# Sliding-window attention followed by a two-layer MLP: a planner that counts engine occupancy and latency apart, no latency between matmuls of one chain, k's copy after q's transposes, identity from the iota

## The chip, the cores and the metric

The kernel runs on one core of one Trainium2 chip. The metric is device microseconds of one execution, as the median over several runs. One execution of each kernel was also profiled. The engines are called PE (TensorE), DVE (VectorE), ACT (ScalarE), POOL (GpSimd) and SP (SyncE).

## The reference, cut to what matters

Eight batches of 576 positions, 8 heads of 64; causal attention in a window of 128 with a linear bias per head, then `relu(x @ w_in)**2 @ w_out` with 512, 2048 and 512 features.

```python
scores = np.matmul(q, k.transpose(0, 1, 3, 2)) / np.sqrt(D)
rel = pos[:, None] - pos[None, :]
mask = (rel >= 0) & (rel < 128)
scores = np.where(mask, scores - slopes[:, None, None] * np.abs(rel), -1e9)   # [B, H, S, S]
attn = softmax(scores)                                                        # cut
x = np.matmul(attn, v).transpose(0, 2, 1, 3).reshape(B * S, H * D)            # 4608 x 512
out = np.square(np.maximum(x @ w_in, 0)) @ w_out                              # 4608 x 512
```

## The kernel before

A block is 128 query positions of one batch (the fifth of each batch has 64), so there are 40 blocks. For each block PE transposes k and q (`tp`), forms scores (`ps_s`), multiplies the probabilities by v (`pv`) and transposes the result (`xp`). For each 512 tokens the MLP makes 16 `h` chains of 4 matmuls and 4 `o` chains of 16. A *chain* here is a row of matmuls that together fill one tile of PSUM, the memory that matmuls write into.

Every instruction group is a `Task`. A list scheduler written in the kernel, `Plan.order`, gives each task a modelled start, and the instructions are recorded in that order. Each engine then works through its instructions in the recorded order on the chip (in the trace of before the 2496 matmuls, 393 instructions of ACT and 579 of DVE stand in the order of the built program); the modelled times themselves do nothing there. The parts that matter:

```python
class Plan:
    LAT = {"PE": 220.0, "ACT": 120.0, "DVE": 120.0, "POOL": 150.0, "SP": 2200.0}
    # ... order(): take the candidate with the earliest start, then the lowest key
                t.end = st + dur + (self.LAT[e] if t.lat is None else t.lat)
            free[e] = st + dur
            # ...
            for u in t.users:
                left[u] -= 1
                u.ready = max(u.ready, t.end)       # also from one matmul of a chain to the next
# ...
    def act(n): return n * 0.833 + 175.0            # ns that ACT is taken
    def dve(n, rate=1): return n / rate / 0.96 + 150.0
    def mm(n): return max(n, 64) / 2.4 + 1.5
# ... attention(m): eight transposes into ONE PSUM tile, k's in its first half, q's in its second
        for i in range(2 * C):
            def emit(i=i):
                # ...
                    slot.tile = psum.tile([128, 1024], BF16, tag=slot.tag, name="tp")
                nc.tensor.transpose(slot.tile[:, i * 128:(i + 1) * 128], ..., ident)
            last = plan.add({"PE": mm(128)}, due - 56, emit, [last, ...], ...)
            if i == C - 1:
                last_k = last
        # ... k's copy, then q's in two halves
        t_k = plan.add(both if first else {"DVE": both["DVE"]}, due - 56, evac_k, [last_k], [], [slot])
        for c2 in range(2):
            t_q.append(plan.add(both if first else {"ACT": both["ACT"]} if c2 else {"DVE": both["DVE"]},
                                due - 56, evac_q, [last, t_zero], [], [slot]))
```

Masks and identity were built on POOL, which also issues all the loads.

The softmax here doesn't subtract the row's maximum and nothing guards it: scores larger than these inputs give would overflow.

## Time and profile before

The time was 366.05 us (median of 3 runs, 364.43 to 366.13). The page's first lines for the kernel before, then its row of PE activity and granted clock in 40 slices of the span (a digit is tenths):

```profile
span 364.2 us, 6535 instructions
...
PE 338.9 (93%) x2496; PEld 187.5 (51%) x2496; DVE 193.8 (53%) x593; ACT 205.1 (56%) x394; POOL 108.4 (30%) x137
...
PE   2677899999999999999999999999999999999995
...
PEclk9996999999999999999999999999999999999999
```

PE is the busy engine, but 93% does not say how much is to be had. The Trainium skill ("Perfetto Trace Analysis", Identifying the Most-Contended Engine) warns that matmul busy time is a poor measure of this, because matmuls are pipelined. So I use another account throughout. At full clock, matmuls of 512, 256, 128 and 65 columns start 216, 110, 56 and 29 ns apart in this trace. At about these pitches (213 for 512) the 2496 matmuls need 317.2 us. **Excess** is what the starts take beyond that:

| stretch, us | excess before, us | named waits of PE in it |
|---|---|---|
| 0 to 60 | 23.3 | loads, copies, exponentials; a clock drop |
| 60 to 300 | 13.6 | 9.7 of it: 29 times a transpose of q waits over 0.1 us for the copy of k |
| after 300 | 1.3 | |

(The prediction counts these waits from 0.2 us on: 27 times and 9.4 us.) With 4.7 us before the first matmul and 4.3 us after the last start, this makes up the span: 4.7 + 317.2 + 38.2 + 4.3 = 364.4 (the last matmul's 0.2 us stand in both 317.2 and 4.3).

The wait of q's transposes is easy to miss. The timeline of PE and DVE at 95 us shows one of them; the columns are start, duration, engine and line, operation, tiles, and shapes:

```profile
95.36 0.22 PE L301 MATMUL tp<-ident,kn_73 128*128 128x128 bf16 x1
95.42 0.38 PE L479 MATMUL o<-w_out_sb,g 128*128 128x512 bf16 x1
...
95.62 0.42 DVE L280 COPY kT_87<-tp 128x512 bf16<-128x512 bf16 x1 [0.23 <-PE tp L301]
95.64 0.38 PE L450 MATMUL h<-xT,w_in_sb 128*128 128x512 bf16 x1
...
96.10 0.22 PE L301 MATMUL tp<-ident,qn_77 128*128 128x128 bf16 x1
```

The `h` matmul that starts at 95.64 is through after 216 ns, at 95.86; the next matmul starts at 96.10, just after the copy of k ends at 96.04. PE lost 0.25 us, and yet no idle time is printed for it, since the modelled duration of the `h` (0.38 us) hides it. Where idle time does show, line 301's view (idle time of its engine, then how often) has it as:

```profile
  DVE kT_86 L280: 1.6, 6
  DVE kT_84 L280: 1.5, 5
  DVE kT_85 L280: 1.0, 4
  DVE kT_87 L280: 0.7, 3
```

That is 4.8 us, where starts show 9.7 in 60 to 300 us alone. The Trainium skill ("PSUM — Partial Sum Buffer", PSUM bank collisions raise a hardware error) says why such a wait is there: engines have to be kept apart by PSUM bank and quarter of the partitions, not by address. k's and q's transposes share one 2 KB tile, and k's copy reads all 128 partitions of it.

### The profile page before, as it was taken

Reading aid. Unit: us, or ns where it says so; the run is one execution under the profiler, and the core shown is the slowest. Engines: PE = TensorE matmul, PEld = TensorE weight load, DVE = VectorE, ACT = ScalarE, POOL = GpSimd, SP = SyncE. Lnnn points to the kernel's source line nnn. Section 1 sums busy time; section 2 is a strip of 40 time slices with the busy share of each in tenths; the row PEclk is TensorE's granted clock in tenths of the full one; section 3 lists DMA queues with packets and bytes.
Section 4 is the critical chain, followed back from the end, with each engine's and each line's share of the span. In section 5 each row is a group of like instructions: output and inputs, shape, how many; then the busy total and the mean of one; then the engine's idle time right before and its main releaser. Section 6 shows DMA issues by size and latency. Waiting matters only on the chain.

```text
span 364.2 us, 6535 instructions
## 1 busy us (share of the span) xinstructions
PE 338.9 (93%) x2496; PEld 187.5 (51%) x2496; DVE 193.8 (53%) x593; ACT 205.1 (56%) x394; POOL 108.4 (30%) x137
## 2 busy tenths in 40 slices
PE   2677899999999999999999999999999999999995
PEld 1454555555555555555555555564555555444442
DVE  4583776476656744566466745664656554322200
ACT  4582775476656754576557645675656643343411
POOL 8967552352444322233243213240100000000000
PEclk9996999999999999999999999999999999999999
DMA  8999999695997967986497777791432000001012
GB/s 56 144 203 160 195 172 86 88 79 60 86 102 51 82 65 76 113 81 40 51 98 70 73 72 75 71 88 36 57 47 38 29 31 31 29 29 58 31 58 87
DMA packets 121951, 28.21 MB, mean 77 GB/s; under 512 B 113216, under 2 KB 117312, under 8 KB 121920
## 3 DMA queue, kind: packets, MB, share of 16 engines
q0 software_dynamic: 116736, 18.36, 68.3%
q1 hardware_dynamic: 5184, 9.44, 7.1%
q8 instruction: 19, 0.31, 0.3%
q14 instruction: 12, 0.10, 0.1%
HBM read 36.70 MB, written 9.44 MB: 127 GB/s over the span
## 4 chain that ended last, share of the span: by engine, by line
PE 76%; issue 7%; POOL 5%; DMA 4%; DVE 4%; ACT 2%; POOLq 0%; ACTq 0%
PE h L450 30%; PE o L479 30%; PE ps_s L337 6%; PE tp L301 5%; PE pv L378 4%; DMA kn_71<-in_k_dram 3%; PE xp L417 2%; DMA qn_74<-in_q_dram 1%; DVE kT_86 L280 1%; DVE kT_87 L280 1%; DVE kT_84 L280 1%; DVE kT_85 L280 1%; POOL w_in_sb L238 1%; POOL kn_70 L262 1%; POOL vt_79 L262 0%
## 5 line engine op out<-in xcount | busy, mean ns | idle before, releaser
L450 PE MATMUL h<-xT,w_in_sb 128*128 128x512 bf16 x576 | 199.4, 382 | 0.7 <-ACT xT L282 0.5
L479 PE MATMUL o<-w_out_sb,g 128*128 128x512 bf16 x576 | 190.8, 379 | 0.2
L458 ACT ACTIVATE rt<-h 128x512 bf16<-128x512 f32 x144 | 85.4, 597 | 84.9 <-PE h L450 69.4
L464 DVE TENSOR_TENSOR g<-rt 128x512 bf16<-128x512 bf16 x144 | 59.8, 419 | 51.3 <-ACT rt L458 49.9
L479 PEld LDWEIGHTS <-g 128*128 128x128 bf16 x576 | 55.2, 98 | 36.0 <-issue 4.7
L450 PEld LDWEIGHTS <-w_in_sb 128*128 128x128 bf16 x576 | 54.8, 98 | 34.8 <-issue 7.0
L399 DVE RECIPROCAL rec<-pv 128x4 f32<-128x4 f32 (+1 forms) x80 | 14.4, 179 | 35.7 <-PE pv L378 34.1
L490 ACT ACTIVATE osb<-o 128x512 f32<-128x512 f32 x36 | 21.5, 596 | 20.7 <-PE o L479 19.9
L355 ACT ACTIVATE P_91<-ps_s 128x512 bf16<-128x512 f32 (+1 forms) x56 | 27.1, 505 | 8.8 <-PE ps_s L337 8.5
L355 ACT ACTIVATE P_92<-ps_s 128x512 bf16<-128x512 f32 (+1 forms) x52 | 26.3, 518 | 8.2 <-PE ps_s L337 7.4
L355 ACT ACTIVATE P_93<-ps_s 128x512 bf16<-128x512 f32 (+1 forms) x52 | 25.9, 515 | 7.2 <-PE ps_s L337 6.5
L378 PEld LDWEIGHTS <-P_91 128*128 128x128 bf16 x200 | 19.1, 98 | 14.4 <-DVE x_94 L404 0.7
L378 PEld LDWEIGHTS <-P_92 128*128 128x128 bf16 x192 | 18.8, 101 | 12.4 <-issue 2.2
L378 PEld LDWEIGHTS <-P_93 128*128 128x128 bf16 x184 | 17.7, 97 | 12.4 <-issue 1.7
L363 DVE TENSOR_TENSOR P_91<-P_91,masks 128x512 bf16<-128x512 bf16 (+1 forms) x56 | 19.7, 361 | 6.5 <-ACT P_91 L355 6.2
L363 DVE TENSOR_TENSOR P_93<-P_93,masks 128x512 bf16<-128x512 bf16 (+1 forms) x52 | 18.7, 365 | 4.8 <-ACT P_93 L355 4.4
L363 DVE TENSOR_TENSOR P_92<-P_92,masks 128x512 bf16<-128x512 bf16 (+1 forms) x52 | 18.4, 365 | 4.9 <-ACT P_92 L355 4.4
L280 DVE COPY xT<-xp 128x512 bf16<-128x512 bf16 (+1 forms) x37 | 14.6, 395 | 8.2 <-PE xp L417 5.8
L417 PE MATMUL xp<-ident,x_94 128*128 128x128 bf16 x80 | 17.5, 224 | 0.0
L417 PE MATMUL xp<-ident,x_95 128*128 128x128 bf16 x80 | 17.1, 223 | 0.0
L404 DVE TENSOR_TENSOR x_94<-pv,rec 128x256 bf16<-128x256 f32 (+1 forms) x40 | 16.7, 416 | 0.5
L262 POOL DMA_DIRECT2D kn_73<-in_k_dram x10 | 8.4, 844 | 28.3 <-PE tp L301 20.9
(99 smaller groups left out, 514.3 us busy)
## 6 DMA issues: line engine op xcount, KB each, us to landing
out_dram<-osb SPq DMA_DIRECT2D x36, 256.0 KB, 2.0
w_in_sb<-in_moe_w_in_dram POOLq DMA_DIRECT2D x4, 512.0 KB, 8.7
w_out_sb<-in_moe_w_out_dram POOLq DMA_DIRECT2D x4, 512.0 KB, 10.8
kn_70<-in_k_dram POOLq DMA_DIRECT2D x8, 128.0 KB, 3.8
qn_74<-in_q_dram POOLq DMA_DIRECT2D x8, 128.0 KB, 4.0
kn_71<-in_k_dram POOLq DMA_DIRECT2D x8, 128.0 KB, 3.6
qn_75<-in_q_dram POOLq DMA_DIRECT2D x8, 128.0 KB, 3.8
kn_72<-in_k_dram POOLq DMA_DIRECT2D x8, 128.0 KB, 3.5
```

What stands on the lines that cost most here:

```text
L280: nc.vector.tensor_copy(o, i)
L301: nc.tensor.transpose(slot.tile[:, i * 128:(i + 1) * 128], src[:, (i % C) * 128:(i % C + 1) * 128], ident)
L337: nc.tensor.matmul(slot_s.tile.rearrange("p (c t q) -> p c t q", c=2, t=2)[:, :, part, 0:n], kT[sk_of[mk].idx][:, c, :], qp[sq.idx][:, c, ...
L355: nc.scalar.activation(view(Pt[sP.idx][:, 2 * c:2 * c + 2]), view(slot_s.tile.rearrange("p (c t q) -> p c t q", c=2, t=2)), AF.Exp, bias=0 ...
L363: nc.vector.tensor_tensor(pt, pt, view(masks[:, 2 * c:2 * c + 2]), op=ALU.mult)
L378: nc.tensor.matmul(slot_v.tile[:, hi * (D + 1):(hi + 1) * (D + 1)], Pt[sP.idx][:, h, part, :], vt[s_in[mk, "v"].idx][:, h, :], start=part ...
L417: nc.tensor.transpose(slot_x.tile[:, c * 128:(c + 1) * 128], xt[sx.idx][:, c * 128:(c + 1) * 128], ident)
L450: nc.tensor.matmul(slot.tile, w_in_sb[:, cc, fc * 128:(fc + 1) * 128], xT[:, cc, g * 512:(g + 1) * 512], start=cc == 0, stop=cc == C - 1)
L458: nc.scalar.activation(srt.tile, slot.tile, AF.Relu, bias=0.0, scale=1.0)
L464: nc.vector.tensor_tensor(sg.tile[:, fc, :], srt.tile, srt.tile, op=ALU.mult)
L479: nc.tensor.matmul(slot.tile, sg.tile[:, fc, t * 128:(t + 1) * 128], w_out_sb[:, fc, :], start=fc == 0, stop=fc == FCB - 1)
L490: nc.scalar.activation(so.tile, slot.tile, AF.Copy)
```

## The change

The intent: let the planner's numbers say what the trace says (how long an engine is *taken*, and how long until a result can be *used*, apart), stop counting latency between matmuls of one chain, start q's transposes without waiting for k's copy, and relieve POOL at the start. In what follows I call the parts A (copy of k), B (planner numbers), C (chain rule) and D (masks and identity).

```diff
-    LAT = {"PE": 220.0, "ACT": 120.0, "DVE": 120.0, "POOL": 150.0, "SP": 2200.0}
+    LAT = {"PE": 260.0, "ACT": 220.0, "DVE": 220.0, "POOL": 200.0, "SP": 2200.0}     # B
+    BEGIN = {"POOL": 1250.0}                                                          # B
-                free.setdefault(e, 0.0)
+                free.setdefault(e, self.BEGIN.get(e, 800.0))                          # B
-                u.ready = max(u.ready, t.end)
+                u.ready = max(u.ready, st + dur if e == "PE" and "PE" in u.engs else t.end)  # C
-        return n * 0.833 + 175.0
+        return n * 0.84 + 55.0                                                        # B
-        return n / rate / 0.96 + 150.0
+        return n / rate / 0.96 + 72.0                                                 # B
-        make_identity(nc, ident)                       # on POOL
-        ... iota and two affine_select on POOL
+        nc.gpsimd.iota(dist, ...)                                                     # D
+        nc.vector.tensor_single_scalar(ident, dist[:, 1], 0.0, op=ALU.is_equal)
+        ... four DVE operations on dist
-            if i == C - 1:
-                last_k = last
-        t_k = plan.add(..., due - 56, evac_k, [last_k], [], [slot])
+        t_k = plan.add(..., due - 56, evac_k, [last], [], [slot])                     # A
-            t1 = plan.add({"DVE": 180.0}, ...
+            t1 = plan.add({"DVE": 97.0}, ...                                          # B
```

More of the change, by code (lines that the diff above doesn't have):

```diff
@@ L6 @@
 import concourse.tile as tile
-from concourse.masks import make_identity
 from concourse._compat import with_exitstack
@@ L160 @@
     dist = const.tile([128, 2, 128], FP32)
+    far = const.tile([128, 2, 128], FP32)
     w_in_sb = const.tile([128, C, d_ff], BF16)
@@ L181, in act, with build_iota, build_ident @@
     def act(n):
-        return n * 0.833 + 175.0
+        return n * 0.84 + 55.0
     def dve(n, rate=1):
-        return n / rate / 0.96 + 150.0
+        return n / rate / 0.96 + 72.0
     def mm(n):
         return max(n, 64) / 2.4 + 1.5
-    def build_consts():
-        make_identity(nc, ident)
-    t_ident = plan.add({"POOL": 800.0}, -9e5 + 0.015, build_consts)
-    def build_dist():
-        pat = [[-128, 2], [1, 128]]
-        nc.gpsimd.iota(dist, pattern=pat, base=128, channel_multiplier=-1,
-                       allow_small_or_imprecise_dtypes=True)
-        nc.gpsimd.affine_select(dist, dist, pattern=pat, channel_multiplier=-1, base=128,
-                                compare_op=ALU.is_ge, fill=1.0e6)
-        nc.gpsimd.affine_select(dist, dist, pattern=[[128, 2], [-1, 128]], channel_multiplier=1,
-                                base=window - 1 - 128, compare_op=ALU.is_ge, fill=1.0e6)
-    t_dist = plan.add({"POOL": 1300.0}, -9e5 + 0.5, build_dist)
+    def build_iota():
+        nc.gpsimd.iota(dist, pattern=[[-128, 2], [1, 128]], base=128, channel_multiplier=-1,
+                       allow_small_or_imprecise_dtypes=True)
+    t_iota = plan.add({"POOL": 360.0}, -9e5 + 0.012, build_iota)
+    def build_ident():
+        nc.vector.tensor_single_scalar(ident, dist[:, 1], 0.0, op=ALU.is_equal)
+    t_ident = plan.add({"DVE": 230.0}, -9e5 - 1, build_ident, [t_iota])
+    def build_dist():
+        mid = (window - 1) / 2.0
+        nc.vector.tensor_single_scalar(far, dist, -mid, op=ALU.add)
+        nc.vector.tensor_tensor(far, far, far, op=ALU.mult)
+        nc.vector.tensor_scalar(far, far, (mid + 0.5) ** 2, 1.0e6, op0=ALU.is_gt, op1=ALU.mult)
+        nc.vector.tensor_tensor(dist, dist, far, op=ALU.add)
+    t_dist = plan.add({"DVE": 1300.0}, -9e5 + 0.5, build_dist, [t_ident])
     t_mask = []
@@ L312, in attention @@
         both = {"ACT": act(C * n), "DVE": dve(C * n, 2)}
-        t_k = plan.add(both if first else {"DVE": both["DVE"]}, due - 56, evac_k, [last_k], [], [slot])
+        t_k = plan.add(both if first else {"DVE": both["DVE"]}, due - 56, evac_k, [last], [], [slot])
         t_q = []
@@ L399, in rec @@
                 nc.vector.reciprocal(srec.tile[0:n, :], pv[0:n, :, D])
-            t1 = plan.add({"DVE": 180.0}, due - 12 + 4 * hf, rec, [last], [srec])
+            t1 = plan.add({"DVE": 97.0}, due - 12 + 4 * hf, rec, [last], [srec])
             def norm(slot_v=slot_v, srec=srec, hf=hf):
```

## The prediction

> **What bounds the kernel.** TensorE. The busy table gives PE 93% of the 364.2 us span, DVE 53%, ACT 56%. In the timeline warm matmuls start 216 ns (512 columns), 110 (256), 56 (128) and 29 ns (65) apart; the Trainium skill ("TensorE: Matmul & The Clock Gate", Back-to-back issue gap) gives N/2.4 + 2.5 ns, which agrees. The 2496 matmuls at about these pitches sum to 317.2 us. The rest of the span: 4.7 us before the first, 4.3 us after the last, 38.3 us of excess between starts. By stretch: 11.1 us before 20 us, 5.1 in 20-30, 4.6 in 30-40, 2.4 in 40-60, 13.6 in 60-300, 1.4 after.
>
> **What the change does.**
> 1. Copy of k after q's transposes. k and q transposes share one 2 KB PSUM tile; before, the copy was recorded between them, so q's transposes wait for it. The Trainium skill ("PSUM — Partial Sum Buffer", PSUM bank collisions) says why such a wait exists. The trace shows PE idle "tp <- DVE kT" 27 times in 60-300 us, 9.4 us together and about 3 us more before. In the built program after no q transpose waits for DVE or ACT. k's copy now starts later, but the first score matmul stands at least 1.28 us of matmul work behind the last transpose from the sixth block on (median over 5 us), so this is mostly hidden. Gain about 10 us, critical.
> 2. Planner durations. Trace: ACT 128x512 starts every 493 ns (model 601 before, 485 after), DVE 128x512 every 334 (417 before, 339 after), last h matmul's start to relu's start 476 ns (213+260 after). The new model fits. Chains run unbroken: the 8 transposes span 0.44 us of PE work instead of 2.1; the first o stands after all 64 first-group h (30 before). This helps the first stage, bounded by latency.
> 3. Identity from the iota, mask distances on DVE. POOL loses a memset and three selects: between q's and the next load it goes from 1.8 us to about 0.5, so all later loads are issued about 1.3 us earlier. DVE gains five small operations (an estimated 1.3 us) while it would wait for data. First transpose near 4.7 us as before (then limited by k's landing, 4.64).
>
> First-stage effect of 2 and 3: first h (before: 29.5 us) at 25-27 us; fewer gaps, maybe without the 0.5 clock granted from 27.7 to 34.6 us. Gain 4-7 us in the first 60 us.
>
> **Sum.** 4.7 + 317.2 + excess (before 60 us: 17 instead of 23; 60-300: 4.5 instead of 13.6; after: 1.4) + 4.3 = 349 us of span; plus 1.8 us that time exceeds span: about 351 us. Range 345.5 to 357. Faster 0.92, within 0.07, slower 0.01.
>
> **What would show it.** "tp <- DVE kT" gone from PE's waits; excess in 60-300 us at most 5 us; first h before 28 us; w_in's last quarter landing near 28.5 us (29.8 before).
>
> **What would make it wrong.** k's and both q copies now stand in a row on one bank (425 + 415 + 591 ns), which the planner thinks parallel; ACT, in order, may stand blocked up to 0.8 us, delaying relus; then PE waits "h <- ACT rt" grow (in 10 of 142 cases an h buffer returns within 1.4 us of PE work). A clock drop in the first 30 us, or PE without work between the 64 h and w_out's landing (40-50 us), costs 3-5 us.

## The result, and the profile after

The kernel after took 350.39 us (median of 4, 349.96 to 350.84) against 366.09 for before in the same comparison: ratio 0.9573, 95% interval 0.9529 to 0.9617. Ratios here are the mean time of one kernel's fast runs over that of the other's of the same rounds, so not quite the ratio of the medians that I quote. All runs in this document are fast (none is over 1.5% above the fastest of its kernel).

The same lines of the page, after:

```profile
span 349.0 us, 6481 instructions
...
PE 329.7 (94%) x2451; PEld 186.9 (54%) x2496; DVE 198.2 (57%) x600; ACT 203.2 (58%) x392; POOL 107.3 (31%) x133
...
PE   2689999999999999999999999999999999999995
...
PEclk9999999999999999999999999999999999999999
```

The busy share of PE moved by one point while the time fell by 4.3%. Note the count: 45 of the 2496 matmul records are missing in this trace (2496 weight loads are there). With them put back, PE would be busy for 332.0 us, 95%. The 317.2 us that the matmuls need went from 87% of the span to 91%, so the skill's warning holds here. A missing record leaves only about 52 ns of idle time, too little for the view of waits, but from start to start it looks like 213 ns lost. I put them back from the order of the built program at their usual pitch; without that, the excess after would read 32.6 us instead of 23.0. The same is done for every kernel below.

| | before | after | difference |
|---|---|---|---|
| excess 0 to 60 us | 23.3 | 17.3 | 6.0 |
| excess 60 to 300 us | 13.6 | 5.2 | 8.4 |
| excess after 300 us | 1.3 | 0.5 | 0.8 |
| span | 364.2 | 349.0 | 15.2 |

The view of busy time by stretch shows where PE gained (columns: stretch, its length, busy time and instructions of PE, PEld, DVE, ACT, POOL, then granted clock, DMA share, GB/s). Before:

```profile
20.00:30.00 10.00, 7.26 (x96) 5.29 (x92) 8.34 (x29) 7.39 (x16) 5.00 (x6) 0.89 1.42 197
30.00:40.00 10.00, 8.48 (x52) 4.49 (x52) 4.39 (x14) 4.63 (x10) 8.85 (x12) 0.77 2.27 163
```

After:

```profile
20.00:30.00 10.00, 8.43 (x98) 6.02 (x98) 7.55 (x28) 7.00 (x15) 3.53 (x5) 1.00 1.53 191
30.00:40.00 10.00, 9.38 (x60) 4.73 (x58) 5.61 (x17) 7.58 (x16) 8.62 (x11) 1.00 2.21 157
```

Before, the granted clock was 0.5 for 6.8 us, from 27.7 to 34.6 us; after, it did not drop once it was full. And k's and q's transposes now stand as two rows of four in the timeline, with no wait between them:

```profile
77.02 0.39 PE L307 MATMUL tp<-ident,kn_74 128*128 128x128 bf16 x4
77.24 0.39 PE L307 MATMUL tp<-ident,qn_78 128*128 128x128 bf16 x4
```

In the view of line 307 no copy of k is left among what PE waited for. So far everything fits the prediction: 350.39 us measured for 351.0 predicted, a span of 349.0 for 349, 8.4 us of steady gain for 9.1. The experiments show that the larger half did not need the cause that it named.

### The profile page after: what moved, and what is told of

Its sections match the earlier page's. It is cut to its first block, busy times and chain, and to the rows that moved or that the text cites. A ratio compares the mean times of both kernels' runs of the same rounds, so it can differ in the third digit from the quotient of the medians.

```text
span 349.0 us, 6481 instructions
## 1 busy us (share of the span) xinstructions
PE 329.7 (94%) x2451; PEld 186.9 (54%) x2496; DVE 198.2 (57%) x600; ACT 203.2 (58%) x392; POOL 107.3 (31%) x133
## 4 chain that ended last, share of the span: by engine, by line
PE 87%; DVE 6%; ACT 5%; issue 1%; ACTq 0%
PE o L483 34%; PE h L454 33%; PE ps_s L341 8%; PE tp L307 5%; PE pv L382 4%; PE xp L421 2%; ACT qp_90 L288 1%; DVE P_92 L367 1%; ACT masks L216 1%; ACT qp_91 L288 1%; ACT rt L462 1%; DVE x_96 L408 0%; ACT P_93 L359 0%; DVE qp_91 L286 0%; ACT P_92 L359 0%
## 5 line engine op out<-in xcount | busy, mean ns | idle before, releaser
L454 PE MATMUL h<-xT,w_in_sb 128*128 128x512 bf16 x557 | 158.7, 379 | 1.0
L483 PE MATMUL o<-w_out_sb,g 128*128 128x512 bf16 x550 | 150.2, 379 | 1.3
L483 PEld LDWEIGHTS <-g 128*128 128x128 bf16 x576 | 54.1, 98 | 51.2
L494 ACT ACTIVATE osb<-o 128x512 f32<-128x512 f32 x36 | 21.5, 597 | 19.1 <-PE o L483 18.8
L367 DVE TENSOR_TENSOR P_92<-P_92,masks 128x512 bf16<-128x512 bf16 (+1 forms) x56 | 20.0, 363 | 8.6 <-ACT P_92 L359 8.2
L403 DVE RECIPROCAL rec<-pv 128x4 f32<-128x4 f32 (+1 forms) x80 | 14.0, 176 | 16.3 <-PE pv L382 15.8
L367 DVE TENSOR_TENSOR P_93<-P_93,masks 128x512 bf16<-128x512 bf16 (+1 forms) x52 | 19.0, 369 | 7.1 <-ACT P_93 L359 6.5
L367 DVE TENSOR_TENSOR P_94<-P_94,masks 128x512 bf16<-128x512 bf16 (+1 forms) x52 | 18.9, 368 | 6.2 <-ACT P_94 L359 5.8
L286 DVE COPY xT<-xp 128x512 bf16<-128x512 bf16 (+1 forms) x39 | 15.3, 393 | 8.5 <-PE xp L421 8.4
L408 DVE TENSOR_TENSOR x_95<-pv,rec 128x256 bf16<-128x256 f32 (+1 forms) x40 | 16.8, 419 | 0.7
L408 DVE TENSOR_TENSOR x_96<-pv,rec 128x256 bf16<-128x256 f32 (+1 forms) x40 | 16.6, 418 | 0.6
L268 POOL DMA_DIRECT2D kn_74<-in_k_dram x10 | 8.5, 845 | 19.7 <-PE tp L307 11.5
L382 PEld LDWEIGHTS <-P_92 128*128 128x128 bf16 x200 | 10.2, 99 | 6.0 <-DVE qp_90 L286 0.7
L268 POOL DMA_DIRECT2D kn_71<-in_k_dram x10 | 8.6, 863 | 14.2 <-PE tp L307 12.1
L268 POOL DMA_DIRECT2D kn_73<-in_k_dram x10 | 8.6, 862 | 13.2 <-PE tp L307 12.1
L382 PEld LDWEIGHTS <-P_93 128*128 128x128 bf16 x192 | 9.8, 101 | 4.7 <-DVE P_93 L367 0.3
```

What stands on the lines that cost most here:

```text
L268: nc.gpsimd.dma_start(o, src[b, :, kb * 128:kb * 128 + n, :].rearrange("h s d -> s h d"))
L367: nc.vector.tensor_tensor(pt, pt, view(masks[:, 2 * c:2 * c + 2]), op=ALU.mult)
L382: nc.tensor.matmul(slot_v.tile[:, hi * (D + 1):(hi + 1) * (D + 1)], Pt[sP.idx][:, h, part, :], vt[s_in[mk, "v"].idx][:, h, :], start=part ...
L408: nc.vector.tensor_tensor(xt[sx.idx][0:n, hf * 256:(hf + 1) * 256].rearrange("p (h e) -> p h e", h=4), pv[0:n, :, 0:D], srec.tile[0:n, :]. ...
L454: nc.tensor.matmul(slot.tile, w_in_sb[:, cc, fc * 128:(fc + 1) * 128], xT[:, cc, g * 512:(g + 1) * 512], start=cc == 0, stop=cc == C - 1)
L483: nc.tensor.matmul(slot.tile, sg.tile[:, fc, t * 128:(t + 1) * 128], w_out_sb[:, fc, :], start=fc == 0, stop=fc == FCB - 1)
```

## The experiments

Twelve kernels ran; all gave correct results. Each was timed in 3 rounds against before. "b_" starts from the kernel before and adds one thing; "a_no" starts from after and takes one part out. The program that would be run was looked at first for how many of the 160 transposes of q wait for a copy: 40 before, 0 after. That this number is 0 for A alone *and* for C alone raised the rival.

Below I go by the intervals, and those of b_A, b_B, b_D and b_Csm leave out 1. Two changed kernels of different rounds are compared by their ratios to before; a_noA's and a_noD's intervals overlap after's, so what A and D are worth within the change is not established.

### b_A: the copy of k alone

```diff
-            if i == C - 1:
-                last_k = last
-        t_k = plan.add(..., evac_k, [last_k], [], [slot])
+        t_k = plan.add(..., evac_k, [last], [], [slot])
```

> The kernel before with one part of the change alone: the copy of k waits for all eight transposes; planner numbers, chain rule and mask building as before. Theory P (the prediction): the wait of q's transposes for the copy of k is gone (none in the built program, 40 before), so 9 to 11 us are gained: 355 to 357.5 us, excess between matmul starts in 60-300 us down from 13.6 to about 4 to 5 us, first 60 us nearly unchanged (22 us of 23.3). Rival R1 (the wait only hid others: in interleaved chains the next wait takes its place): 360 us or more, with a new PE wait of several us in 60-300 us.

Measured: 361.61 us, ratio 0.9887 (0.9835 to 0.9938). Excess 23.0 before 60 us and 8.9 in 60 to 300 us. R1 held: all 29 steady waits of q's transposes are gone, 9.7 us of them, but the steady excess fell by 4.8 us only. Before, 5 gaps over 100 ns that were not this wait took 1.1 us in 60 to 300 us; here 21 such gaps take 5.8 us, spread over many causes (the longest 0.78 us, `pv` waiting for DVE's write of x).

In the first stage 4.6 us of waits for k's copy vanished and next to nothing was gained (23.0 for 23.3), and there the trace shows most of the reason. PE's timeline of this kernel:

```profile
27.38 0.19 PE L376 MATMUL pv<-vt,P 128*128 128x65 bf16 x1
30.67 0.50 PE L301 MATMUL tp<-ident,kn 128*128 128x128 bf16 x3 [3.10 <-DMA kn<-in_k_dram]
30.97 0.63 PE L448 MATMUL h<-xT,w_in_sb 128*128 128x512 bf16 x1
31.39 0.31 PE L301 MATMUL tp<-ident,kn 128*128 128x128 bf16 x1
```

PE came earlier to the transposes of the sixth block, whose k landed no earlier, and waited 3.1 us for it. In all, waits for loads grew from 2.9 to 6.1 us in the first 60 us, and waits for copies of q from 5.5 to 7.4.

### b_C: the chain rule alone

```diff
-                u.ready = max(u.ready, t.end)
+                u.ready = max(u.ready, st + dur if e == "PE" and "PE" in u.engs else t.end)
```

> The kernel before with the chain rule alone (no latency between matmuls of one chain). In the built program its q transposes wait for no copy either (0 of 160, 40 before), since the unbroken eight are recorded ahead of the copy. Theory P reads parts 1 and 2 as separate gains: about 10 us by the moved copy, a few us of the first stage by the rest, so this alone would give 2 to 4 us: 362 to 364. Rival R2 (either part removes the same wait, the two overlap): 353 to 357 us, and excess in 60-300 us about 5 us.

Measured: 350.36 us, ratio 0.9564 (0.9520 to 0.9608): the time of the whole change, from one line. Below even R2's range. Excess 17.3 before 60 us, 3.9 in 60 to 300 us; no clock drop; no wait for k's copy. The first lines of its page:

```profile
span 347.5 us, 6485 instructions
...
PE 326.5 (94%) x2451; PEld 185.2 (53%) x2496; DVE 193.9 (56%) x592; ACT 203.6 (59%) x395; POOL 108.5 (31%) x137
```

### a_noA and a_noC: the change without the copy, and without the chain rule

```diff
 a_noA, against after:
-        t_k = plan.add(..., evac_k, [last], [], [slot])
+        t_k = plan.add(..., evac_k, [last_k], [], [slot])     # last_k as before
 a_noC, against after:
-                u.ready = max(u.ready, st + dur if e == "PE" and "PE" in u.engs else t.end)
+                u.ready = max(u.ready, t.end)
```

> The kernel after with the copy of k released after k's own four transposes again. Theory P: the wait comes back, 358 us or more. Rival R2: the unbroken chain of eight keeps the wait away by itself (0 of 160 in the built program), so 349 to 352 us, the same as after within 1%, with no PE wait tp <- DVE kT.

Measured: 353.01 us, ratio 0.9640 (0.9597 to 0.9682), in the same rounds as b_A, b_C and a_noC. No wait for k's copy came back, so Theory P fell: the copy's move is not needed for that. It is 1 us outside R2's range. The steady excess is 6.6 us against 5.2; A would be worth 2.6 us beside the other parts (353.01 against 350.39, with intervals that overlap).

> The kernel after with the latency inside matmul chains again (chains interleave as before), all else changed. Theory P: the first stage loses its shorter chains, so 2 to 4 us: 352 to 355 us, all of the difference in the first 60 us; excess in 60-300 us stays about 5 us. Rival R3 (unbroken chains are what serves the steady stage): 356 us or more with excess in 60-300 us up by several us.

Measured: 366.06 us, ratio 1.0002 (0.9949 to 1.0054). Three of the four parts together, A, B and D, gave **nothing**. The excess of 60 to 300 us is 14.1, none of it waits for k's copy: PE waits for copies of q, for osb, for relu, for x, 36 gaps over 100 ns with 10.8 us. R3 held, Theory P fell by over 10 us.

### b_B: the planner numbers alone

```diff
+    LAT, BEGIN, act(), dve() and the 97 ns of the reciprocal as in the change; nothing else
```

> The kernel before with the planner's new durations, latencies and start times alone; chains still interleave and q's transposes still wait for the copy of k (40 waits in the built program). Theory P: numbers that fit the trace better help a little, 362 to 366 us. Theory C (now leading, after the chain rule alone gave 350.4 us and after without it 366.1 us: only unbroken chains matter): the new numbers without the chain rule give nothing or cost a few us, 365 to 371 us, with the tp <- DVE kT waits of about 9 us still there in 60-300 us.

Measured: 369.73 us, ratio 1.0082 (1.0056 to 1.0109): slower by 0.8%. Steady excess 17.5 us; waits for k's copy are 6.5 us of it (25 over 0.1 us), less than the 9 that I expected, with 7.6 us of others. Numbers that fit the trace made the order worse. The built programs show one way: the eight transposes of a block span 3.3 us of PE work here and 2.1 before. With the latency inside chains still counted, a longer one stretches them: the kernel before with PE's latency alone raised from 220 to 260 (built, not run) has 3.2.

### b_D: masks and identity alone

```diff
+    iota on POOL; identity and distances from it on DVE, as in the change; nothing else
```

> The kernel before with the masks' distances and the identity built the new way, alone. Theory P: loads are issued 1.3 us earlier and 1 us at most is gained: 364.5 to 366 us. Theory C: nothing beyond 1%, 363 to 369 us. Both: w_in's last quarter lands within 0.3 us of 29.8 us although it is issued 1.3 us earlier, as in after, if its landing is set by the transfers.

Measured: 363.96 us, ratio 0.9934 (0.9897 to 0.9972). The first stage gained 4.1 us of excess (19.2), the steady stage lost 1.6. Part of the 4.1 is the clock, which did not drop in this trace and did in before's. The last quarter of w_in landed at 28.59 us, not within 0.3 of 29.8, so that expectation of both theories was wrong. Over all 14 profiled kernels this landing is 29.7 to 31.1 us where POOL builds the masks (8 kernels, mean 30.3) and 28.6 to 29.7 where it does not (6 kernels, mean 29.2). The 1.3 us of earlier issue do come out at the landing on the mean; before (29.78) and after (29.72) happen to lie at the near ends of the two groups.

### a_noB and a_noD: the change without the planner numbers, and without the new masks

```diff
 a_noB, against after: LAT, no BEGIN, act(), dve() and 180 ns for the reciprocal as before
 a_noD, against after: make_identity, iota and both affine_select on POOL as before
```

> The kernel after with the old planner numbers (chain rule, moved copy and new mask building kept). Theory P: worse numbers cost some of the first stage, 352 to 354 us. Theory C: 349 to 351 us, as after or slightly better; excess in 60-300 us 4 to 5 us.

Measured: 347.56 us, ratio 0.9468 (0.9434 to 0.9502): faster than after, with an interval that does not meet after's. Both ranges were missed on the good side. Steady excess 3.1 us, first stage 15.8.

> The kernel after with the old mask and identity building on POOL. Theory P: all loads 1.3 us later, so 351 to 352.5 us. Theory C: 349 to 352 us; the first h matmul within 1 us of after's 27.9 us.

Measured: 352.06 us, ratio 0.9592 (0.9560 to 0.9623), which both ranges held. The first `h` started at 30.0 us (after: 27.9), so here Theory P was the closer one: D would be worth about 1.7 us, in the first stage (excess 19.0 against 17.3).

### b_Ctp, b_Cho, b_Csm: which chains?

The rule of C for some chains alone; each PE task carries the name of its chain.

```diff
-                u.ready = max(u.ready, t.end)
+                u.ready = max(u.ready, st + dur if t.kind == u.kind and t.kind in KINDS else t.end)
```

KINDS is the transposes of k and q (b_Ctp), `h` and `o` (b_Cho), or `ps_s`, `pv` and `xp` (b_Csm). With all six kinds the built program is b_C's.

> The kernel before with the chain rule for the transposes of k and q alone. In the built program 1 of 160 q transposes waits for a copy (40 before). Theory T (unbroken transposes do all the work): 350 to 354 us. Theory S (several chains matter; moving the copy alone, which removes the same wait, gave 361.6 us): 357 to 362 us, tp <- DVE kT gone, and 3 to 5 us of other waits in 60-300 us as when the copy alone was moved.

Measured: 356.11 us, ratio 0.9730 (0.9697 to 0.9763). Between the ranges, closer to S: the waits for the copy are gone in the steady stage (excess 5.9), the first stage keeps 21.5 us.

> The kernel before with the chain rule for the h and o matmuls alone; 40 q transposes still wait for the copy. Theory T: 364 to 368 us, nothing gained. Theory S with h and o as the lever (whole groups evacuated one at a time): 360 us or less, though tp <- DVE kT stays at about 9 us in 60-300 us.

Measured: 364.20 us, ratio 0.9975 (0.9923 to 1.0027): nothing outside the interval, steady waits for the copy 10.4 us. `h` and `o` by themselves are not the lever.

> The kernel before with the chain rule for the small chains of the attention (scores, P times v, transposes of x) alone; 40 q transposes still wait. Theory T: 364 to 368 us. Theory S with the small chains as the lever in the first stage, which waits for latency: first 60 us lose 19 us or less instead of 23.3, and 360 to 363 us.

Measured: 358.85 us, ratio 0.9809 (0.9779 to 0.9840), better than I expected from the first stage alone: excess 19.4 there, and 10.1 in the steady stage, where waits for the copy still take 7.1 us.

The three medians lie 10.1, 2.0 and 7.4 us below before, 19.5 in sum, where all together gave 15.7; the gains overlap. The transposes serve the steady stage, the small chains the first stage and a quarter of the same waits (9.7 to 7.1 us).

### a_bank: telling the plan of the shared bank

In after, the plan believes that k's copy and the two copies of q can run side by side on DVE and ACT. They read one PSUM tile, and in the built program a semaphore wait stands between copies on different engines, so they run in a row. A place in after's timeline (DVE's copy of k follows ACT's copy of q; the first scores follow DVE's copy of q):

```profile
89.36 0.59 ACT L288 ACTIVATE qp_91<-tp 64x512 bf16<-64x512 bf16 x1
89.99 0.42 DVE L286 COPY kT_86<-tp 128x512 bf16<-128x512 bf16 x1 [0.64 <-ACT qp_91 L288]
...
90.66 0.41 DVE L286 COPY qp_91<-tp 64x512 bf16<-64x512 bf16 x1
...
90.88 0.19 PE L382 MATMUL pv<-vt_83,P_93 128*128 128x65 bf16 x1
91.13 0.28 PE L341 MATMUL ps_s<-qp_91,kT_85 128*128 128x256 bf16 x1
```

DVE stood still for 0.64 us in front of a copy that was its next instruction, and PE then waited 0.2 us beyond its pitch for the last copy.

```diff
-                                due - 56, evac_q, [last, t_zero], [], [slot]))
+                                due - 56, evac_q, [last, t_zero, t_q[0] if c2 else t_k], [], [slot]))
```

> The kernel after, but the plan is told that k's copy and q's two copies read one PSUM bank and follow one another (each depends on the one before[...]). Theory M (the new planner numbers cost 2.8 us because the old ones, being too long, covered for this row of copies): 347 to 349 us, PE waits <- DVE qp in 60-300 us down from 1.4 us to under 0.5 us, excess there 3 to 4 us. Rival L (the loss is scattered order luck or lies in the first stage): 350 to 352 us.

Measured: 344.77 us (344.23 to 345.35), ratio 0.9420 (0.9389 to 0.9450), the fastest kernel here: its interval lies below after's, and just meets a_noB's (0.9434 to 0.9502). It went past Theory M's range. PE's waits as the view of waits has them (total, times, longest), for copies of q, after:

```profile
PE ps_s L341 <- DVE qp_90 L286: 1.7, 2, 1.4
PE ps_s L341 <- DVE qp_89 L286: 1.5, 2, 1.3
...
PE ps_s L341 <- ACT qp_91 L288: 0.9, 1, 0.9
...
PE ps_s L341 <- DVE qp_91 L286: 0.7, 2, 0.5
...
PE pv L382 <- DVE qp_90 L286: 0.2, 1, 0.2
```

and in a_bank, where the buffers of a ring carry one name:

```profile
PE ps_s L341 <- DVE qp L286: 1.9, 3, 1.3
...
PE ps_s L341 <- ACT qp L288: 1.3, 1, 1.3
```

That is 5.0 us against 3.2. In 60 to 300 us, counted by starts, after had 7 gaps over 100 ns with 2.0 us; a_bank has none. The rest of the gain is in the first stage, where Theory M had none and Rival L put the loss without expecting it back: excess 12.9 against 17.3, first `h` at 25.7 us against 27.9. PE in the first stage of a_bank, by stretch:

```profile
20.00:30.00 10.00, 9.19 (x86) 5.36 (x88) 7.90 (x30) 6.58 (x15) 3.59 (x6) 1.00 1.56 192
30.00:40.00 10.00, 9.95 (x80) 6.02 (x79) 7.33 (x23) 8.23 (x18) 8.64 (x11) 1.00 2.17 159
```

Theory M says two things. That the unmodelled row of copies costs time under the new numbers is shown by this run for the steady stage: the 1.4 us of PE's waits for copies of q there are gone, and the excess is 2.3 us less. For the first stage it is not shown: waits for copies of q fell from 5.7 to 4.1 us, which is 1.6 of the 4.4 us gained, and part of the rest may be the clock (below). That the *old* numbers were better because their padding covered for the row is only argued; a_noB with the same dependence would test it and was not run.

## Why the prediction was right, and where its reasons were wrong

**The total was right** (350.39 for 351.0), and so was the account of where time would go: excess before 60 us 17.3 for 17, in 60 to 300 us 5.2 for 4.5, span 349.0 for 349. The waits for k's copy vanished, the clock drop vanished, w_in was issued 1.3 us earlier. The first `h` came at 27.9 us, under the 28 it was to be under but later than the 25 to 27 of the sum. That the total came out so near is partly luck: it counted 9.1 us for a wait whose removal by A alone took 4.8 us off the excess, and what C did to the other waits, of which it said nothing for the steady stage, made up the rest.

**Part 1, "Gain about 10 us, critical", was laid at the wrong part.** The wait was real and it did go, but moving the copy alone is worth 4.4 us (366.03 to 361.61), and the change without it still has no such wait (353.01 us). The failed step is "In the built program after no q transpose waits for DVE or ACT", read as the work of part 1. The built program of after has four parts in it; b_C's program shows the same zero. When all eight transposes are recorded without a break, the copy comes behind them by itself. And removing a wait of 9.7 us did not give 9.7 us, because with interleaved chains other waits grew by 4.7 us (1.1 to 5.8), and in the first stage waits for loads took back most of it (about 3.3 of 4.6 us).

**Part 2 put B and C in one point and valued both wrongly.** "The new model fits" is true of single instructions: ACT 128x512 starts every 493 ns in the trace against 485 in the model. Yet B costs: 3.5 us alone (369.73 against 366.26) and 2.8 us within the change (350.39 against 347.56). "This helps the first stage" was said of unbroken chains, which are in fact the whole: C alone 350.36, all but C 366.06.

Why C does it is shown in part. First, it removes the waits for the copy. Second, interleaved chains wait for each other, since PE takes matmuls in recorded order. Before, the timeline of PE at 29 us has

```profile
29.48 0.58 PE L450 MATMUL h<-xT,w_in_sb 128*128 128x512 bf16 x1 [0.47 <-ACT xT L282]
30.71 0.29 PE L301 MATMUL tp<-ident,kn_71 128*128 128x128 bf16 x1 [0.64 <-DMA kn_71<-in_k_dram]
30.79 0.26 PE L378 MATMUL pv<-vt_82,P_92 128*128 128x65 bf16 x1
30.86 0.62 PE L450 MATMUL h<-xT,w_in_sb 128*128 128x512 bf16 x1
...
31.45 0.62 PE L450 MATMUL h<-xT,w_in_sb 128*128 128x512 bf16 x1
```

By the order of the built program the `h` at 30.86 opens another chain, and the one at 31.45 is the second of the first chain. It needs the same tokens and the same quarter of w_in as the first, which had run at 29.48; it started 2.0 us later, behind a transpose whose data were still on their way. After, the first chain has no stranger in it (the first line holds the three records left of its four matmuls, and the first of the next chain):

```profile
27.93 1.24 PE L454 MATMUL h<-xT,w_in_sb 128*128 128x512 bf16 x4
29.01 0.39 PE L421 MATMUL xp<-ident,x_95 128*128 128x128 bf16 x4
29.23 4.91 PE L454 MATMUL h<-xT,w_in_sb 128*128 128x512 bf16 x22
```

That the rule is also *true* shows in the same traces: within unbroken `o` chains, which accumulate into one tile, matmuls start 216 ns apart (median of some 350 pairs after), the pitch of unrelated ones. Before, the plan put other work into a latency that does not exist, and stretched eight transposes from 0.44 to 2.1 us of PE work. How the remaining steady gain splits between fuller PSUM slots and bursts on ACT and DVE, no run here separates.

**Part 3 was right in kind.** D measured 1.7 us within the change (intervals overlap) and 2.3 us alone (0.7%, interval 0.3 to 1.0%), where loads are issued 1.3 us earlier. The single landing that was to show it (28.5 us) was measured at 29.72; kernels scatter by about a microsecond there.

**The risk that was named, copies in a row on one bank, was real.** Planning for it gave 5.6 us (350.39 to 344.77, medians of different rounds, ratios 0.9573 and 0.9420 to before), of which only the steady part is tied to the copies. I had it as ACT standing blocked and relus late; PE's waits for relu after were 0.2 us, and it was the scores that waited. "Mostly hidden" holds for the steady stage, where planning for the row took 2.3 us off the excess; 4.4 us came off in the first stage, with the cause open in part.

**The clock drop.** The Trainium skill ("TensorE: Matmul & The Clock Gate", What's actually happening) has a gate with two states, full and half, decided in windows of about 3.4 us. Traces agree: granted 1.0 or 0.5 only, with drops of 3.4 or 6.8 us between 23 and 37 us, in before and in six of the twelve experiments, and in neither after nor a_bank as profiled. In the runs of before that were made beside a_bank, those with a mean granted clock of 1.00 took 364.4 to 365.6 us, the others (0.988 to 0.995) 366.2 to 366.7 us. The drop goes with 1 to 2 us (the prediction feared 3 to 5), a part of the 6 us of the first stage.

One thing the profile's page does not show. The clock's records begin at 17.5 us in before, 21.1 in after and 14.8 in a_bank, and that page prints full clock ahead of them. The starts say half, as in after (timeline of PE, 20.5 to 21.6 us):

```profile
20.65 0.58 PE L421 MATMUL xp<-ident,x_96 128*128 128x128 bf16 x4
21.06 0.40 PE L307 MATMUL tp<-ident,kn_71 128*128 128x128 bf16 x4
21.29 0.39 PE L307 MATMUL tp<-ident,qn_75 128*128 128x128 bf16 x4
```

Four transposes take 0.41 us in the first row and 0.23 in the second; the single ones start 107 ns apart up to 20.95 us and 56 ns apart from 21.12 us on. If none of it hides in a wait, the matmuls before the first record lost 3.0 us in before, 5.0 in after and 2.7 in a_bank by this (an estimate, from their number and the two pitches). So up to 2.3 of the 4.4 us that a_bank gained in the first stage may be an earlier full clock. Whether the order of the program or the single run sets that moment, one profile of each kernel cannot say.

## What to carry to other kernels

Take a bundle apart before crediting its parts: here one line out of four changes made all of the gain, and two routes removed the same wait. In a planner for in-order engines, the structure (which tasks truly wait for which, chains without latency, readers of one bank in a row) was worth far more than exact durations, and the numbers that fit the trace made things worse, by 3.5 us alone and by 2.8 within the change. Count a pipelined engine's losses from start to start; the printed idle time showed less than half of the wait that mattered.

## What the Trainium skill lacked or had wrong

- "TensorE: Matmul & The Clock Gate", Back-to-back issue gap: it puts the sustained pitch of streams in which each matmul has its own weight load at about 81 ns (128 columns) and 131 ns (512), and calls N/2.4 + 2.5 the isolated figure. Here, with a weight load for every matmul, 128 columns start 56 ns apart and 512 columns 216 ns (median of 1083 after, least 215): the formula holds for the stream, as another part of the page has it, and those two figures do not.
- The same page (Single matmul latency) gives 379 ns for 512 columns by its formula (the records, whose ends are modelled, have a median of 379), but does not say that matmuls accumulating into one tile do not wait for each other: 216 ns apart within a chain as outside. Counting that latency inside chains cost this planner 15.7 us.
- "PSUM — Partial Sum Buffer" says that engines must be kept apart by bank and quarter of the partitions, but not what it does to a schedule. Here three copies of one bank by two engines run in a row, q's two as well, which read different halves of the partitions; planning for the row took 2.3 us off the steady excess, and 5.6 us off the time with what came along in the first stage.
- No page that I used says how far an earlier issue of loads is seen at their landing: issued 1.3 us earlier, w_in landed 1.1 us earlier on the mean, with a spread of 1.1 to 1.4 us among kernels of one group.
